# Three edits at the two edges of a hash-attention and MLP kernel: order and form of the projection requests, the buffer ring of the last output quarters, and wider unused products

## The chip, the cores and the metric

The kernel runs on one core of a Trainium2 chip. The metric is the device time of one execution in microseconds (us), median of several runs. In all the tables "trace" is one profiled execution; its span leaves out about 1.8 us that the timed figure has (898.2 against 899.9 for the kernel before), so spans are compared with spans and times with times.

## The reference, cut to what matters

```python
# q, k, v: (4, 8, 768, 64); proj: (64, 6); w_in: (512, 2048); w_out: (2048, 512); all float32
q_bits = (einsum('bhsd,dk->bhsk', q, proj) > 0)
k_bits = (einsum('bhsd,dk->bhsk', k, proj) > 0)
mask   = bucket(q_bits)[:, :, :, None] == bucket(k_bits)[:, :, None, :]
attn   = softmax(where(mask, q @ k.T / sqrt(64), -1e9))
x      = (attn @ v) -> (3072 tokens, 512)
out    = relu(x @ w_in) ** 2 @ w_out
```

The kernel goes through 16 pairs of heads and then through the two large products in chunks of tokens. The change touches only the first 12 us (the first pair's way from DRAM to its first scores) and the last 12 us (the way of the last output block to DRAM).

## The kernel before

The first loads and the start of the program. `nc.sync` is SyncE (SP), `nc.scalar` ScalarE (ACT), `nc.vector` VectorE (DVE), `nc.gpsimd` GpSimd (POOL); a `dma_start` on one of them is a request that this engine's sequencer issues.

```python
def load_first():
    for src, name in ((q, "q_nat"), (k, "k_nat")):
        t = p_qk.tile([P, SB, 2, D], FP32, name=name)
        for h, queue in enumerate((nc.sync, nc.scalar)):
            queue.dma_start(out=t[:, :, h], in_=src[0, h].rearrange("(t p) d -> p t d", t=SB))
        if src is q:
            nc.scalar.dma_start(
                out=projs[:, 0:NBITS],
                in_=proj.rearrange("(o d) n -> o d n", o=1).to_broadcast([2, D, NBITS]),
            )
        nat[0, name] = t

def keep_busy(n, w=512):            # products that nobody reads: they hold TensorE's clock up
    for _ in range(n):
        nc.tensor.matmul(out=void[:, 0:w], lhsT=busy[:, 0:P], rhs=busy[:, 0:w], start=True, stop=True)

# ... (cut)
load_first()
keep_busy(8)
# ... (constants, further loads: cut)
first_features(0, 0)                # TensorE transposes of the queries, copy out of PSUM
first_features(0, 1)
keep_busy(2, 256)
first_features(1, 0)                # transposes of the keys, first half
hash_bits(0, turn("hash"), (0,))    # needs projs
signs(0, 0)
first_keys(0, turn("hash"))
first_features(1, 1)
keep_busy(4)
```

The last outputs. `put_out` serves all output blocks but one; `put_last` serves the two quarters of the last block, which is finished after everything else.

```python
def put_out(i, ih, jh, n, o):
    ot = p_y.tile([P, HN], FP32, name="ot", bufs=2)
    nc.vector.transpose(out=ot, in_=o)
    # ... (cut)
    for a in range(P // 32):
        queue = nc.gpsimd if (ih, jh) == (1, 1) else nc.sync
        if (i, ih, jh) == (NCHUNK - 1, 1, 0) and a % 2:
            queue = nc.gpsimd
        queue.dma_start(out=out[at, ...], in_=ot[a * 32:(a + 1) * 32]...)   # cut

def put_last(n, o):
    row, col = n // 2, n % 2
    # ... (two TensorE transposes into PSUM: tp; cut)
    ot = p_y.tile([P, HN], FP32, name="ot", bufs=2)[:, 0:QN]
    if col:
        nc.scalar.copy(out=ot, in_=tp)
    else:
        nc.vector.tensor_copy(out=ot, in_=tp)
    # ... (cut)
    (nc.sync if col else nc.scalar).dma_start(out=out[lo:lo + QN, ...], in_=ot...)
```

## Time and profile before

| mark in the trace of before | us |
|---|---|
| time, median of 3 runs (range) | 899.87 (899.56 to 900.54) |
| span of the trace | 898.2 |
| first key transposes start on TensorE | 8.47 |
| first hash product | 8.91 |
| first score product | 12.28 |
| last TensorE work (transposes of the last quarters) starts | 887.93 |
| last copy starts, on DVE | 892.92 |
| GpSimd's closing drain ends | 895.37 |
| last store lands | 895.98 |

Read it as two edges around a full middle. TensorE computes nothing that counts before the keys are there, and after the last transposes another 10.3 us (898.2 - 887.93) pass in copying, storing and closing. "First score product" is the best mark for the front: a delay ahead of it moves all that follows. "Span minus start of the last transposes" is the best mark for the back.

### The profile page before, as it was taken

How to read it: one execution, taken by the hardware profiler on the slowest of the kernel's cores; microseconds unless marked ns; L12 is line 12 of the kernel's file. 1: busy time of each engine (PE TensorE's matmuls, PEld its weight loads, DVE VectorE, ACT ScalarE, POOL GpSimd, SP SyncE). 2: the span in 40 equal slices, each digit the busy share in tenths (PEclk: the TensorE clock that was granted, in tenths of full speed). 3: DMA queues.
4: the chain of work that ended last, by engine and by line, in shares of the span. 5: the costliest groups of instructions: out<-in, count | busy, mean ns of one | idle time of the engine just before them, and what ended most of it. 6: DMA issues, size and time to landing. Idle time of an engine off the chain costs nothing.

```text
span 898.2 us, 11774 instructions
## 1 busy us (share of the span) xinstructions
PE 878.5 (98%) x4296; PEld 502.8 (56%) x4296; DVE 711.0 (79%) x991; ACT 376.6 (42%) x609; POOL 91.7 (10%) x148
## 2 busy tenths in 40 slices
PE   8999999999999999999999999999999999999994
PEld 3444444444444444444688854446888544458883
DVE  4899999998999986888778775568777755777784
ACT  4988878887888861222211112222111122221110
POOL 2000000000000000554000111112001111100002
PEclk9999999999999999999999999999999999999998
DMA  9577879898976325999855744447757344445564
GB/s 180 104 149 145 198 176 208 166 274 204 265 158 159 107 100 205 292 267 288 314 171 154 180 85 141 128 148 274 242 153 191 63 144 152 153 138 156 152 180 81
DMA packets 219969, 158.14 MB, mean 176 GB/s; under 512 B 163746, under 2 KB 180642, under 8 KB 219906
## 3 DMA queue, kind: packets, MB, share of 16 engines
q1 hardware_dynamic: 186752, 84.04, 38.8%
q10 hardware_dynamic: 22418, 37.76, 13.9%
q0 software_dynamic: 10736, 35.53, 13.1%
q8 instruction: 36, 0.59, 0.3%
q14 instruction: 27, 0.22, 0.1%
HBM read 119.28 MB, written 38.01 MB: 175 GB/s over the span
## 4 chain that ended last, share of the span: by engine, by line
PE 90%; DVE 4%; DMA 3%; ACT 1%; issue 1%; SPq 0%; DVEq 0%; ACTq 0%
PE acc L688 58%; PE st L397 16%; PE xo L426 13%; PE tot L445 2%; PE hash L347 2%; DMA out_dram<-ot 1%; DVE total L416 1%; DMA raw<-in_moe_w_out_dram 1%; ACT bits L357 1%; DMA k_nat<-in_k_dram 1%; DVE peaks L729 0%; DVE b L778 0%; DVE ot L842 0%; DVE h L777 0%; DVE b_t L504 0%
## 5 line engine op out<-in xcount | busy, mean ns | idle before, releaser
L688 PE MATMUL acc<-x,w_unit 128*128 128x512 f32 x384 | 169.3, 592 | 0.0
L401 ACT ACTIVATE e<-st 128x1024 f32<-128x1024 f32 x192 | 145.2, 810 | 49.6 <-PE st L397 45.2
L397 PE MATMUL st<-feat,feat 64*128 64x512 f32 (+1 forms) x768 | 150.3, 483 | 0.0
L426 PE MATMUL xo<-e,v_nat 128*64 128x512 f32 (+1 forms) x768 | 134.8, 492 | 0.0
L688 PE MATMUL acc<-b,leaf 128*128 128x256 f32 x600 | 132.9, 379 | 0.0
L688 PE MATMUL acc<-t_x,w_unit 128*128 128x512 f32 x288 | 127.8, 593 | 0.0
L688 PEld LDWEIGHTS acc<-x,w_unit 128*128 128x128 f32 x384 | 72.9, 190 | 90.5 <-issue 89.9
L688 PEld LDWEIGHTS acc<-b,leaf 128*128 128x128 f32 x600 | 114.0, 190 | 16.8 <-issue 1.4
L416 DVE TENSOR_TENSOR total<-total,e 128x1536 f32<-128x1536 f32 x58 | 101.9, 1757 | 3.8
L426 PEld LDWEIGHTS xo<-e,v_nat 128*64 128x64 f32 x768 | 51.4, 136 | 82.4 <-issue 74.9
L688 PEld LDWEIGHTS acc<-t_x,w_unit 128*128 128x128 f32 x288 | 54.5, 190 | 69.7 <-issue 67.5
L397 PEld LDWEIGHTS st<-feat,feat 64*128 64x128 f32 x768 | 66.0, 188 | 33.9 <-issue 25.3
L777 DVE TENSOR_TENSOR h<-acc,two 128x512 f32<-128x512 f32 x24 | 16.6, 691 | 83.9 <-PE acc L688 83.8
L695 ACT COPY two<-acc 128x512 f32<-128x512 f32 (+1 forms) x45 | 21.9, 487 | 132.7 <-PE acc L688 116.8
L688 PE MATMUL acc<-t,leaf 128*128 128x256 f32 x336 | 76.5, 380 | 0.3 <-DVE t L504 0.3
L357 ACT ACTIVATE bits<-hash,lifts 32x384 bf16<-32x384 f32 x124 | 71.0, 573 | 7.6 <-PE hash L347 4.4
L695 ACT COPY one<-acc 128x512 f32<-128x512 f32 (+1 forms) x45 | 21.9, 487 | 113.1 <-PE acc L688 63.6
L688 PEld LDWEIGHTS acc<-t,leaf 128*128 128x128 f32 x336 | 63.6, 190 | 9.8 <-DVE t L504 1.1
L778 DVE SCALAR_TENSOR_TENSOR b<-h 128x512 f32<-128x512 f32 x96 | 64.3, 690 | 2.5
L397 PE MATMUL st<-bits,bits 64*128 64x256 bf16 (+1 forms) x384 | 63.1, 325 | 2.1 <-ACT e L401 1.2
L688 PE MATMUL acc<-b_t,leaf 128*128 128x256 f32 x240 | 54.5, 380 | 1.8 <-issue 1.8
L688 PEld LDWEIGHTS acc<-b_t,leaf 128*128 128x128 f32 x240 | 45.3, 190 | 9.0 <-issue 3.0
(127 smaller groups left out, 869.1 us busy)
## 6 DMA issues: line engine op xcount, KB each, us to landing
leaf<-w_out ACTq DMA_DIRECT2D x142, 256.0 KB, 3.0
w_unit<-w_in SPq DMA_DIRECT2D x24, 896.0 KB, 4.7
raw<-in_moe_w_in_dram SPq DMA_DIRECT2D x16, 512.0 KB, 5.6
raw<-in_moe_w_out_dram SPq DMA_DIRECT2D x16, 512.0 KB, 4.6
w_out<-sums POOLq DMA_DIRECT2D x16, 448.0 KB, 7.1
v_nat<-in_v_dram SPq DMA_DIRECT2D x16, 384.0 KB, 4.3
x_all<-x_t SPq DMA_DIRECT2D x16, 384.0 KB, 3.0
x<-x_all POOLq DMA_DIRECT2D x3, 2048.0 KB, 12.1
```

The source lines that it names most:

```text
L347: nc.tensor.matmul(out=banks[g * NR_B:(g + 1) * NR_B, h, 0:HS], lhsT=projs[rows], rhs=feat[pr, w][rows, c * HS:(c + 1) * HS], start=True, ...
L357: nc.scalar.activation(out=t[h * D:h * D + NR_B, c * HS:(c + 1) * HS], in_=hashed[pr, w][at, h, 0:HS], func=ACTF.Sign, scale=HUGE, bias=li ...
L397: nc.tensor.matmul(out=st[:, h, 0:hi - lo], lhsT=src[pr, 1][rows, key], rhs=src[pr, 0][rows, lo:hi], start=first, stop=not first,)
L401: nc.scalar.activation(out=e[:, :, lo:hi], in_=st[:, :, 0:hi - lo], func=ACTF.Exp, scale=scale)
L416: nc.vector.tensor_tensor(out=totals[pr], in0=totals[pr], in1=weights[pr, kt][:, :, 0:S], op=ALU.add)
L426: nc.tensor.matmul(out=xo[h * D:(h + 1) * D, lo:hi], lhsT=nat[pr, "v_nat"][:, h, kt * D:(kt + 1) * D], rhs=weights[pr, kt][:, h, lo:hi], s ...
L445: nc.tensor.matmul(out=tot[g * 32:(g + 1) * 32, 0:HS], lhsT=ones, rhs=src[:, h, c * HS:(c + 1) * HS], start=src is srcs[0], stop=src is sr ...
L688: nc.tensor.matmul(out=acc[to], lhsT=a(i), rhs=b(i), start=first and i == 0, stop=last and i == n - 1, skip_group_check=True,)
L695: nc.scalar.copy(out=t, in_=acc[of])
L777: nc.vector.tensor_tensor(out=h, in0=one, in1=two, op=ALU.add)
L778: nc.vector.scalar_tensor_tensor(out=out[:, r], in0=h, scalar=0.0, in1=h, op0=ALU.max, op1=ALU.mult)
```

## The change

It has three parts: the projections are asked for behind the keys, one plain 64 x 6 request on each of the two queues in place of one broadcast request on ACT's; the two unused products between queries and keys are 512 columns wide instead of 256; the last two output quarters take their buffers from another ring, which is idle by then.

```diff
-            if src is q:
-                nc.scalar.dma_start(
-                    out=projs[:, 0:NBITS],
-                    in_=proj.rearrange("(o d) n -> o d n", o=1).to_broadcast([2, D, NBITS]),
-                )
             nat[0, name] = t
+        for h, queue in enumerate((nc.sync, nc.scalar)):
+            queue.dma_start(out=projs[h * D:(h + 1) * D, 0:NBITS], in_=proj)
...
-        keep_busy(2, 256)
+        keep_busy(2)
...
-            ot = p_y.tile([P, HN], FP32, name="ot", bufs=2)[:, 0:QN]
+            ot = p_r.tile([P, HN], FP32, name="h", bufs=3)[:, 0:QN]
```

## The prediction

> **What bounds the kernel now.** I read the page first (busy shares, then the chain of work that ended last), then the chain in order of time, then the timeline of the first 12 us and the last 30 us, because the diff touches nothing in between.
>
> ```profile
> span 898.2 us, 11774 instructions
> PE 878.5 (98%) x4296; PEld 502.8 (56%) x4296; DVE 711.0 (79%) x991; ACT 376.6 (42%) x609; POOL 91.7 (10%) x148
> PE 90%; DVE 4%; DMA 3%; ACT 1%; issue 1%; SPq 0%; DVEq 0%; ACTq 0%
> ```
>
> TensorE is the bound: busy in 98% of the span and 90% of the chain. A change that takes no product away can only gain where TensorE has not begun yet or has already ended, so the two edges are what matters. The chain in order of time shows both edges:
>
> ```profile
> 2.67 5.66 DMA k_nat<-in_k_dram
> 8.47 0.52 PE tp L310 x3
> ...
> 887.45 0.59 DVE o L828 x2
> 888.04 4.80 DMA out_dram<-ot
> 892.92 0.42 DVE ot L866
> ```
>
> At the front one transfer, half of the first pair's keys, holds the whole program until 8.47 us. At the back the program waits 4.8 us for an output transfer before one 0.42 us copy. The timeline of the front (start, duration, engine, line; "ACTq" is an issue of a transfer by ScalarE's sequencer):
>
> ```profile
> 1.29 0.53 SPq L270 DMA_DIRECT2D k_nat<-in_k_dram  x1
> 1.50 1.14 ACTq L274 DMA_DIRECT2D projs<-in_proj_dram  x1
> 2.67 0.39 ACTq L270 DMA_DIRECT2D k_nat<-in_k_dram  x1
> 6.15 0.63 PE L327 MATMUL xo<-busy 128*128 128x256 bf16 x2
> 8.47 0.52 PE L310 MATMUL tp<-ident,k_nat 128*128 128x128 f32 x3 [1.69 <-DMA k_nat<-in_k_dram]
> ```
>
> SP asks for its half of the keys at 1.29 us. ACT asks for the other half only at 2.67 us, because it asks for the projections first, and that one request takes 1.14 us of issuing. TensorE is through with the queries and the two unused products at 6.78 us (6.15 + 0.63) and is idle 1.69 us until the ACT half has landed. From issue to landing, by the list of transfers (KB, us): the SP half 4.5 us, so at 5.8; the ACT half 5.7 us, so at 8.35.
>
> ```profile
> k_nat<-in_k_dram SPq DMA_DIRECT2D x1, 192.0 KB, 4.5
> k_nat<-in_k_dram ACTq DMA_DIRECT2D x1, 192.0 KB, 5.7
> ```
>
> The back:
>
> ```profile
> 887.93 0.77 PE L859 MATMUL acc<-ident,o 128*128 128x128 f32 x4 [1.09 <-DVE o L828]
> 888.40 0.37 ACT L864 COPY ot<-acc 128x256 f32<-128x256 f32 x1 [5.47 <-PE acc L859]
> 888.80 0.39 SPq L868 DMA_DIRECT2D out_dram<-ot  x1
> 892.92 0.42 DVE L866 COPY ot<-acc 128x256 f32<-128x256 f32 x1 [4.72 <-DMA out_dram<-ot]
> 893.38 0.40 ACTq L868 DMA_DIRECT2D out_dram<-ot  x1
> ```
>
> The last two output quarters take the same path (transpose on TensorE, copy out of PSUM, store), one through ACT and SP, one through DVE and ACT. The first finds a free buffer. The second draws the ring of two "ot" buffers round to the one that the transposed block of 886.40 us still occupies, and whose last piece GpSimd asked for only at 888.04; it lands at 892.85, and the copy starts at 892.92 although its input was ready at 888.70 (887.93 + 0.77).
>
> **What the Trainium skill says.** (1) "DMA: Bandwidth & Descriptors", section "Why a DMA increments its semaphore by 16 and not by 1": the slowest dimension of both sides decides over how many of the 16 DMA engines a transfer is spread; "Rules for kernel authors" there warns that a leading broadcast of c copies confines it to c engines. The old projection request has a leading broadcast of 2, so 128 descriptors of 24 bytes would sit on two engines, ahead of the keys in ACT's queue; the new ones have 64 partitions outermost, 4 descriptors for each engine. No view here shows engines singly, but the 1.14 us issue (0.39 to 0.53 for the larger ones) and the 5.7 against 4.5 us of the two key halves agree. (2) Same page, "Issuing engines are not separate DMA queues": asking from two queues saves issue time only, since both share the 16 engines. So I expect earlier requests, not more bandwidth. (3) "TensorE: Matmul & The Clock Gate", Part 1: the array runs at half clock until it has been busy for about 3.4 us, in a free-running window. The trace agrees:
>
> ```profile
> L310 PE MATMUL tp<-ident,q_nat x6: 421/421/421, 4.9 to 5.9; 128*128 128x128 f32 x6
> L310 PE MATMUL tp<-ident,k_nat x6: 272/273/330, 8.5 to 10.7; 128*128 128x128 f32 x6
> ```
>
> The transposes of the queries, to 6.36 us, ran at the low clock (421 ns), those of the keys from 8.47 at the high one (272 ns); the change of clock fell between. (4) "DMA: Bandwidth & Descriptors", "Anatomy of one DMA": about 2 us of a small transfer is fixed, mostly the receipt of the write. Here the 128 KB store that ran alone took 2.6 us, and the one at 888.80 that shared the engines took 4.2.
>
> **The change, part by part.**
>
> Projections behind the keys. ACT's key request moves from 2.67 to about 1.3 us, beside SP's. Bandwidth: the two queries and two key halves are 4 x 192 KB = 786 kB; the list of rates shows up to 285 GB/s while both queues carry such rows, from about 2.05 us on. 786 / 275 = 2.9 us, so the last byte comes at about 4.95; the queries landed 0.65 to 1.1 us after their last bytes by the same count, so both key halves land at about 5.6 to 6.0 us, against 8.35. The projections, 3 KB, follow in both queues and should land by 6.5. They are wanted by the hash, after the key transposes, so they get no wait of their own unless they land after about 7.4.
>
> Two unused products of 512 columns in place of 256. At the low clock one takes about 0.43 us (eight took 3.59 at 1.48 us), so TensorE is through at 6.15 + 0.86 = 7.0 instead of 6.6 us. They now become what the keys wait for: key transposes at 7.0 instead of 8.47, 1.47 us earlier. They are there so that the clock is up by then; if it rises later, three transposes at double spacing cost 0.25 us more and the first hash about as much. I take 0.15 off: front gain 1.3 us. It stays: from there each step of the first pair waits for compute (ACT signs, exponentials, DVE sums), not for a transfer, and the first idle time that a transfer ends, the weights at 204.5 us, is counted from an SP request that itself waited for DVE. Everything moves up together.
>
> Quarters in the ring "h". That ring (three buffers) was last used by the gates long before, and the built program confirms that the two copies keep only their wait for TensorE; the two pieces of SP and of GpSimd drop out of it. The DVE copy moves from 892.92 to about 888.75, its store from 893.38 to about 889.2, 4.1 us earlier. Not all of it counts: the GpSimd piece still lands at 892.85 and SP's store at 888.80 + 4.2 = 893.0, and the new store shares the engines with both. Its 128 KB at some 180 GB/s is 0.7 us more, so the last landing is at 893.0 to 893.7 instead of 895.98 (893.38 + 2.6). After the last landing come 2.2 us (898.2 - 895.98) of closing semaphores, unchanged. Gain 2.3 to 2.9 us, if nothing else ends later.
>
> Sum: 1.3 + 2.5 = 3.8 us.
>
> **The rivals.**
>
> Rival A: GpSimd's closing drain sets the new end.
>
> ```profile
> L1254 POOLq DRAIN  x3: 40/113/6670, 888.7 to 897.9; - x3
> ```
>
> The first of these begins at 888.7 and lasts 6.67 us, to 895.37. I do not know what ends it. If it follows GpSimd's own transfers, the change leaves it where it is; the closing exchange then takes the 0.8 us from 897.4, where GpSimd's closing semaphores begin, to 898.2, the end is at 896.2 before the front gain, and the back gain is 2.0 and not 2.7. For it: its start depends on nothing that the change moves. Against it: it may end with the last store of all. I give it a half, hence 2.5 in the sum. Time if true: 896.6.
>
> Rival B: the keys gain little, because the projections or the pair-1 loads now stand in the way. For it: one wait for the projections is now on both queues, and SP asks for 96 KB loads from about 2.3 us on. Against it: those are behind the keys in SP's queue, and the projections are small and spread. Front gain 0.7; time 896.7.
>
> Rival C: the clock is still low at 7.0 us, and stays so for up to a microsecond more, since the window runs free. Front gain 0.8; time 896.6.
>
> Rival D: both edges give their best (1.5 and 2.9): 895.5.
>
> Rival E: a gap of the front is taken up later, where something not moved sets the pace. Against it: after 340 us the chain is products of TensorE nearly without a gap, and before it each wait is relative. Time 897.4 with only the back gain.
>
> **Range and chances.** 899.87 - 3.8 = 896.1 us, taking the difference of spans as the difference of times. The three runs of before lie within 1.0 us, so I widen beyond D and B: 895.0 to 897.4. 2% is 18 us, more than both edges together hold (8.5 us ahead of the keys, some 10 us after the last product), so faster by 2% has 0.005 and slower, for which I see no mechanism, 0.005.
>
> **What would show it.** Right: ACT's key request at about 1.3 us and both halves landed by about 6; key transposes starting at 6.8 to 7.2 us right behind the unused products, with no wait for a transfer; the hash without one for the projections; the DVE copy at about 888.8 less the front gain, waiting for TensorE; the last landing about 2.5 us earlier against the last product. The step on the clock is judged by the 421 or 272 ns of the key transposes. The drain of GpSimd, its end counted from the copy of L864, decides between A and my first sum. Wrong would be: a wait of more than 0.3 us for the projections or the keys after 7.2 us, a middle stretch that is longer than before, or a time outside 895.0 to 897.4.

## The result

The changed kernel takes 895.67 us (median of 6 runs, 894.87 to 896.34), the kernel before in the same rounds 899.65 us (897.04 to 900.54). The ratio is 0.9958, with an interval of 0.9945 to 0.9972. Here and below a ratio is the mean time of one kernel's runs over that of the other's runs in the same rounds, so it isn't quite the ratio of the medians. The spans of the two traces differ by 4.3 us (898.2 - 893.9).

The page of the changed kernel, span and shares of the chain:

```profile
span 893.9 us, 11767 instructions
...
PE 92%; DVE 4%; DMA 1%; ACT 1%; issue 1%; SPq 0%; ACTq 0%; DVEq 0%
```

The transfers' share of the chain fell from 3% to 1%, but not by the change alone. The 4.8 us output transfer at the back has left the chain. About half of the fall is a weights transfer of 7.60 us at 204.5 us, in the middle stretch that is examined below. The keys are still on the chain, now from 1.29 to 6.64 us instead of 2.67 to 8.33:

```profile
1.29 5.35 DMA k_nat<-in_k_dram
6.69 0.55 PE tp L307 x3
```

The front in the timeline (start, duration, engine, line, count, and in brackets the idle time before it with what ended it):

```profile
1.29 0.67 ACTq L270 DMA_DIRECT2D k_nat<-in_k_dram  x1
...
5.78 0.59 PE L324 MATMUL xo<-busy 128*128 128x512 bf16 x2
...
6.69 0.55 PE L307 MATMUL tp<-ident,k_nat 128*128 128x128 f32 x3 [0.31 <-DMA k_nat<-in_k_dram]
...
7.26 1.46 PE L344 MATMUL hash<-feat,projs 64*32 64x384 f32 x12
```

ACT asks for its half of the keys at 1.29 instead of 2.67 us. The wait of 1.69 us has shrunk to 0.31. The unused products are through at 6.37 (5.78 + 0.59), the keys come at 6.69, and the hash follows the key transposes (6.69 + 0.55 = 7.24) without a gap. The transfers of this front (KB, us from issue to landing):

```profile
k_nat<-in_k_dram ACTq DMA_DIRECT2D x1, 192.0 KB, 5.4
...
projs<-in_proj_dram SPq DMA_DIRECT2D x1, 1.5 KB, 5.3
```

So ACT's keys land at 6.7 (1.29 + 5.4), and projections of 1.5 KB need 5.3 us behind the keys (ahead of them, in an experiment below, 3.1 to 3.4): asked for at 1.87 and 2.00, they land at 7.2 to 7.3, with nothing to spare before the hash. The back:

```profile
885.57 0.77 PE L856 MATMUL acc<-ident,o 128*128 128x128 f32 x4 [1.09 <-DVE o L825]
...
886.38 0.42 DVE L863 COPY h<-acc 128x256 f32<-128x256 f32 x1 [0.53 <-PE acc L856]
```

The DVE copy waits for TensorE alone, 0.53 us, where it waited 4.72 us for a store. Its own store is asked for at 886.83. GpSimd's closing drain, in the list of instructions by line (shortest, median and longest in ns; first and last start):

```profile
L1251 POOLq DRAIN  x3: 40/112/6770, 886.3 to 893.7; - x3
```

Its long instance, 6.77 us from 886.3, ends at 893.07, and the span ends 0.83 us later. In the kernel before it ended at 895.37, only 0.6 us ahead of the last landing. Now the two lie further apart: the last landing is at about 891.0 (886.83 + 4.2), and the drain is what comes last.

Where the 4.3 us of the two traces came from, by the marks:

| stretch | before | after | difference |
|---|---|---|---|
| start to first score product | 12.28 | 10.53 | 1.75 |
| from there to the first product of the second block | 327.91 | 327.22 | 0.69 |
| from there to the last transposes | 547.74 | 547.82 | -0.08 |
| from there to the end | 10.27 | 8.33 | 1.94 |

The 0.69 us in the middle is examined below; it isn't the change's.

### The profile page after: what moved, and what is told of

The parts are those of the page before. It is cut to its first block, busy times and chain, and to the rows that moved or that the text cites. A ratio compares the mean times of both kernels' runs of the same rounds, so it can differ in the third digit from the quotient of the medians.

```text
span 893.9 us, 11767 instructions
## 1 busy us (share of the span) xinstructions
PE 878.5 (98%) x4296; PEld 502.5 (56%) x4296; DVE 710.9 (80%) x991; ACT 376.0 (42%) x609; POOL 91.5 (10%) x148
## 4 chain that ended last, share of the span: by engine, by line
PE 92%; DVE 4%; DMA 1%; ACT 1%; issue 1%; SPq 0%; ACTq 0%; DVEq 0%
PE acc L685 58%; PE st L394 17%; PE xo L423 14%; PE tot L442 2%; PE hash L344 2%; DVE total L413 1%; DMA k_nat<-in_k_dram 1%; ACT bits L354 1%; DMA out_dram<-ot 0%; DVE peaks L726 0%; DVE b L775 0%; DVE ot L839 0%; DVE h L774 0%; DVE b_t L501 0%; ACT e L398 0%
```

## The experiments

My theory after the result: the front gains because ACT's keys are asked for earlier, which comes from the short issue of the new request as much as from its place; the back gains 2 us because the wait for a buffer is gone, and would gain more if GpSimd's drain did not end last. Rivals: the unused products (through the clock) make the front's gain; the back's gain is the whole gain and the front's is absorbed; the end follows the last store, not the drain. Twelve runs, of ten new kernels and the two known ones, were made in three groups on three chips. All gave correct results, and all the timed runs were in the fast state; the single look at the kernel before has no state. The last column of the table gives the two marks of the edges, from one trace of each kernel.

| kernel | median us (before, same rounds) | ratio (95%) | first score product; last transposes to end |
|---|---|---|---|
| last ring alone | 897.70 (899.98) | 0.9969 (0.9956 to 0.9981) | 12.94; 8.41 |
| projections alone | 898.44 (899.98) | 0.9980 (0.9967 to 0.9993) | 10.77; 10.18 |
| wide products alone | 899.32 (899.98) | 0.9988 (0.9976 to 0.9999) | 12.21; 10.41 |
| old request, behind the keys | 898.24 (899.98) | 0.9981 (0.9968 to 0.9994) | 11.06; 10.22 |
| full change again | 895.90 (900.33) | 0.9949 (0.9936 to 0.9961) | 10.88; 8.45 |
| full change, narrow products | 896.34 (900.33) | 0.9954 (0.9941 to 0.9967) | 10.41; 8.36 |
| full change, ACT stores for GpSimd | 894.64 (900.33) | 0.9946 (0.9932 to 0.9959) | 10.60; 7.01 |
| three ideas together | 893.54 (900.33) | 0.9922 (0.9910 to 0.9935) | 10.73; 7.05 |
| eight wide products, before | 898.69 (900.26) | 0.9988 (0.9971 to 1.0004) | 12.54; 10.55 |
| new request, ahead of the keys | 898.02 (900.26) | 0.9982 (0.9966 to 0.9997) | 10.53; 10.63 |
| three ideas, no unused products | 892.83 (900.26) | 0.9916 (0.9902 to 0.9930) | 9.73; 6.72 |
| before again, one look | 899.59 | (single run, state unknown) | 13.33; 10.37 |

**The last ring alone.** The kernel before with the last part of the change only:

```diff
-            ot = p_y.tile([P, HN], FP32, name="ot", bufs=2)[:, 0:QN]
+            ot = p_r.tile([P, HN], FP32, name="h", bufs=3)[:, 0:QN]
```

> The kernel before with only the last quarters in the ring h. Theory of the drain: the DVE copy follows the transposes at once (about 888.8 us instead of 892.9) and the last store lands 2 to 3 us earlier, but GpSimd's closing drain keeps its start (888.7) and its 6.7 us, so it ends at about 895.4 and the span at 896.2: gain 2.0 us, about 897.7 us, ratio 0.9978. Theory that the last store alone sets the end: last landing about 893.3 plus 2.2 us, span 895.5, gain 2.7 us, ratio 0.9970. Theory that the wait only moves elsewhere: under 0.5 us.

Its ratio is 0.9969, so 2.8 us. In the trace the stretch after the last transposes is 8.41 us, as in the full change and 1.86 less than before; the drain ends at 895.15 and the span 0.85 later. So the back's gain stands by itself and is bounded by the drain. The span is 2.2 us shorter than that of before: 1.86 at the back, 1.0 in the middle (0.63 of it ahead of the second block, examined below), and 0.66 lost at the front, where nothing was edited and yet the first score product came at 12.94 instead of 12.28. The reason is in the front of this trace:

```profile
8.11 0.87 PE L310 MATMUL tp<-ident,k_nat 128*128 128x128 f32 x3 [2.41 <-DMA k_nat<-in_k_dram]
```

Three key transposes took 0.87 us where they took 0.52 in before. The view by stretches (us; busy time of TensorE, its weight loads, DVE, ACT, POOL, each with a count; granted clock, the share of full speed that TensorE was allowed; DMA share; GB/s) says why, first for this kernel:

```profile
8.00:10.00 2.00, 1.89 (x13) 0.89 (x15) 0.56 (x1) 0.00 (x0) 0.00 (x0) 0.50 1.56 143
```

and then for the kernel before:

```profile
8.00:10.00 2.00, 1.53 (x15) 0.60 (x15) 0.56 (x1) 0.11 (x1) 0.00 (x0) 1.00 1.34 133
```

In the idle stretch of 2.41 us, 2.2 us after its start, the granted clock fell to half, where it stayed from about 7.9 to 11.3 us, and this run did 13 products in these two microseconds where the other did 15. Here TensorE was through with queries and unused products at 5.70 us, against 6.78 in before (its clock had risen sooner: six query transposes took 0.82 us against 1.49), and so waited longer for keys that came at nearly the same time. What it won early, it lost again at half clock. (The view shows a clock of 1.00 from the start in every trace here, though the first eight products plainly ran slow. So the low clock of the first microseconds is read from durations, and only the later falls from the records.)

**The kernel before again.** To see whether that was chance, the unchanged kernel was looked at a second time.

> The kernel before once more, for its trace: from the first sign activation to the first product of the second block 328.8 us if the weights of 204 us happen to land in time, up to 330.3 if not; half clock after the keys if the window falls badly, not otherwise; back edge as before: 10.2 to 10.4 us from the last transposes to the end.

```profile
8.48 0.52 PE L310 MATMUL tp<-ident,k_nat 128*128 128x128 f32 x3 [1.94 <-DMA k_nat<-in_k_dram]
...
8.93 2.21 PE L347 MATMUL hash<-feat,projs 64*32 64x384 f32 x12
...
13.33 0.39 PE L397 MATMUL st<-bits,bits 64*128 64x512 bf16 x2
```

The same program, with the keys at the same time (8.48 against 8.47), waited 1.94 us instead of 1.69, ran at half clock from about 9.6 to 13.0, took 2.21 us for a hash that takes 1.5, and reached its first score product 1.05 us later. So the kernel before has two fronts, 12.3 and 13.3 us, by chance. The Trainium skill ("TensorE: Matmul & The Clock Gate", section "Why this matters for your kernels") advises to leave no gaps over about 3 us between bursts of products, since one window of idle puts the clock back to half. The clock records here agree on the half clock, and both spells of it lasted 3.41 us; but they came with only 1.94 and 2.41 us of idle, and with 1.69 us in a third run there was none. The length of the idle time can't be the whole rule: in this run the clock fell at 9.57 us, when TensorE had been busy again for 1.09 us. What decides between the cases was not tested. In none of the nine traces of kernels with early keys did the clock drop after the queries: their idle ahead of the keys was 1.11 us at most.

**The projections alone.** The first part of the change on the kernel before.

```diff
-            if src is q:
-                nc.scalar.dma_start(out=projs[:, 0:NBITS], in_=...to_broadcast([2, D, NBITS]))
+        for h, queue in enumerate((nc.sync, nc.scalar)):
+            queue.dma_start(out=projs[h * D:(h + 1) * D, 0:NBITS], in_=proj)
```

> The kernel before with only the projections asked for behind the keys on both queues (unused products 256 wide as before). Theory of the request order: ACT's key half is asked for at 1.3 us and lands at about 6.6, key transposes start at about 6.7 instead of 8.5, gain 1.5 to 1.8 us, ratio about 0.9982; TensorE waits some 0.3 us longer for the keys than in the full change, nothing else differs. Rival, that the wider unused products carry part of it by lifting the clock: key transposes at 421 ns and a gain of 1.0 us or less.

It takes 0.9980 of the time before, 1.8 us, and its first score product comes at 10.77, against 12.28 or 13.33. The back is as before (10.18 against 10.27). The front's gain is real by itself; with the ring's 2.8 us it makes 4.6 us, and the full change makes 3.8 us in the first measurement and 4.6 us (0.0051 x 900) in its repeat below. Within the intervals, about 1.1 us to each side, the two edges add, and no absorption of the front's gain is to be seen. The first key transposes did run at low clock here (three took 0.90 us, against 0.55 in the full change), the sign that the rival had named, but the gain isn't the 1.0 us or less that it expected with that sign.

**Old request behind the keys, and new request ahead of them.** The first part changes two things at once: the place of the request and its form. One kernel moves the old broadcast request behind the keys:

```diff
-            if src is q:
-                nc.scalar.dma_start(out=projs[:, 0:NBITS], in_=...to_broadcast([2, D, NBITS]))
             nat[0, name] = t
+        nc.scalar.dma_start(out=projs[:, 0:NBITS], in_=...to_broadcast([2, D, NBITS]))
```

> The kernel before with the old single broadcast request for the projections, but placed behind the keys on ACT's queue. If the order of the requests is all that matters: the keys land at about 6.6 us, gain 1.5 us, ratio 0.9983. If the form matters too (128 small pieces on few engines, 1.14 us to issue): the projections land clearly after the keys (later than 7.5 us), the first hash waits for them, and the gain is 0.3 to 1.0 us.

The other keeps the old place and takes the new form:

```diff
             if src is q:
-                nc.scalar.dma_start(out=projs[:, 0:NBITS], in_=...to_broadcast([2, D, NBITS]))
+                for h, queue in enumerate((nc.sync, nc.scalar)):
+                    queue.dma_start(out=projs[h * D:(h + 1) * D, 0:NBITS], in_=proj)
```

> The kernel before with the projections still asked for ahead of the keys, but in the new form, one request of 64 rows on each queue. If the form alone does it (short issue, spread pieces): ACT's keys are asked for at about 1.9 instead of 2.67 us and land at about 7.1, SP's 0.6 later than before at 6.4: key transposes at about 7.1, gain 1.2 to 1.4 us, nearly that of the full front. If it is the order: keys land after 8 us, gain under 0.4 us.

The old request behind the keys:

```profile
8.30 0.87 PE L346 MATMUL hash<-feat,projs 64*32 64x384 f32 x12 [0.74 <-DVE feat L318]
```

The keys were transposed from 7.01 on, but the hash began only at 8.30: TensorE stood 0.74 us. The profile puts the wait down to the DVE copy of the keys, which ended at 8.15. But the first hash products use the queries alone: in the changed kernel they start at 7.26, when that copy had not even begun. So what they waited for is the projections, whose request was issued from 1.99 to 3.13 us. (This is inferred: the list of transfers gives no landing for this one.) The new request ahead of the keys:

```profile
2.07 0.59 ACTq L270 DMA_DIRECT2D k_nat<-in_k_dram  x1
...
10.53 0.39 PE L395 MATMUL st<-bits,bits 64*128 64x512 bf16 x2 [0.46 <-ACT bits L355]
```

Its two projection requests took 0.54 and 0.58 us of issue instead of 1.14, ACT's keys were asked for at 2.07 and landed 4.2 us later, at 6.3, *earlier* than in the full change, where they were asked for at 1.29 and needed 5.4 us. SP's half came later instead, and it is the half that TensorE waited for:

```profile
2.12 0.82 SPq L270 DMA_DIRECT2D k_nat<-in_k_dram  x1
...
k_nat<-in_k_dram SPq DMA_DIRECT2D x1, 192.0 KB, 4.5
...
6.72 0.52 PE L308 MATMUL tp<-ident,k_nat 128*128 128x128 f32 x3 [1.11 <-DMA k_nat<-in_k_dram]
```

Both halves were there at 6.6 to 6.7 us, as in the full change. The projections took 3.4 us at most. The first score product is at 10.53, the same as in the full change. In time the two are alike (0.9981 and 0.9982, both some 1.7 us), and like the projections alone (0.9980), so the times don't tell the three apart. (For the old request behind the keys 0.3 to 1.0 us was expected: the wait for the projections came, the smaller gain didn't show in the time.) In the traces, one of each, the form of the request is enough for the gain, the order alone gets less at the mark (11.06), and both together get no more than the form; but the full change's own two traces lie at 10.53 and 10.88. Asking for ACT's keys 0.8 us sooner did not bring the last half of the keys sooner: 6.7 us in both. And "form" is itself two things: the broadcast is gone, and the rows are split over two queues. The two new requests take 1.12 us of issue together, as much as the old one's 1.14, but side by side on SP and ACT. A split request that keeps the broadcast, or a plain one on ACT alone, was not run, so which of the two helps stays open.

**The wide products alone**, in the kernel before:

```diff
-        keep_busy(2, 256)
+        keep_busy(2)
```

> The kernel before with only the two unused products widened from 256 to 512 columns. Theory of the request order: the keys still land at about 8.35 us, TensorE is idle 1.3 instead of 1.7 us before them, gain 0.0 us, ratio 1.000. Rival (clock): the clock is up earlier and the first pair runs faster, gain 0.3 us or more.

The ratio is 0.9988 with an interval that ends at 0.9999, and the mark at the front is 12.21, 0.07 from that of before. A mean gain of a microsecond fits a kernel that no longer falls to half clock in some of its runs (its idle ahead of the keys was 1.46 us, and the clock held), but one trace and this interval don't show it.

**Eight wide products** in their place were to fill nearly the whole wait:

```diff
-        keep_busy(2, 256)
+        keep_busy(8)
```

> The kernel before with eight unused products of 512 columns where it has two of 256, enough to keep TensorE busy nearly until the keys land at 8.35 us. The trace of ring_only showed the clock granted at half from 7.9 to 11.3 us, after 2.4 us of idle before the keys; before itself did not show it. Theory that the wait for the keys sometimes costs the clock: no half clock after the keys in this run, mean 0.3 to 0.8 us under before, and a narrower spread than before has. Theory that the half clock is rare or costs nothing: within 0.3 us of before. If the eight end after the keys have landed (clock low throughout): up to 0.4 us slower.

The idle ahead of the keys was 1.06 us, the clock held, the first score product came at 12.54, and the ratio is 0.9988 (0.9971 to 1.0004): unclear. How often the kernel before runs at half clock, and so what unused products are worth there on average, stays open.

**The full change again, and with the narrow products.** The first is the changed kernel unedited; the second is it with

```diff
-        keep_busy(2)
+        keep_busy(2, 256)
```

> The full change once more, as the yardstick for the other three runs on this chip. About 3.8 us under before, ratio 0.9958; GpSimd's closing drain starts at about 886.3 us, lasts 6.7 to 6.8 us and ends 0.8 us before the span does. Any middle stretch (from the first sign activation to the first product of the second block) between 328.8 and 330.3 us, as in the traces so far, would be chance of the transfers.

> The full change with the two unused products put back from 512 to 256 columns. Theory that the width does nothing once the keys come early: same time as the full change within 0.3 us; TensorE idle about 0.7 instead of 0.3 us before the keys, clock not falling since that gap is short. Rival, that the wider products are what keeps the clock up: in some runs the half clock lasts over the first hash (key transposes at 421 ns), mean 0.4 to 0.8 us slower and a wider spread than the full change.

The repeat measured 0.9949 and the narrow one 0.9954, medians 895.90 and 896.34, with intervals that overlap nearly whole. In the repeat the clock was still low during the unused products (0.81 us for two), and the keys began at 7.04 right behind them; in the narrow one the products took 0.38 us and the keys began at 6.57. The narrow one's first score product is earlier by 0.47 us (10.41 against 10.88), which the times don't show. The second part of the change does nothing measurable once the keys come early.

The repeat also settles the middle stretch. DVE's wait for a weights transfer in it and in the kernels before and after is given in brackets, in the timeline near 210 us; first before:

```profile
212.12 0.43 DVE L141 TENSOR_SCALAR power<-raw 128x512 uint32<-128x512 uint32 x1 [1.53 <-DMA raw<-in_moe_w_out_dram]
```

and then the repeat:

```profile
210.61 0.43 DVE L141 TENSOR_SCALAR power<-raw 128x512 uint32<-128x512 uint32 x1 [1.34 <-DMA raw<-in_moe_w_out_dram]
```

The wait was 1.53 us in one trace of the kernel before and nothing in the other; it was 0.70 us in one trace of the changed kernel and 1.34 in the other. One program shows both, so the 0.69 us that the middle of the first pair of traces differs by is chance and not the change.

**ACT stores for GpSimd's last two.** The full change, with the two pieces of the last `put_out` that GpSimd asked for given to ACT:

```diff
                 if (i, ih, jh) == (NCHUNK - 1, 1, 0) and a % 2:
-                    queue = nc.gpsimd
+                    queue = nc.scalar
```

> The full change with the two pieces of the last transposed block that GpSimd stored now stored from ACT's queue, so that GpSimd comes to its closing drain some 2.5 us earlier. Theory that the drain takes about 6.7 us from when GpSimd arrives and has been the end: it starts at about 883.8, ends at about 890.5, and the end is again the last landing (about 891) plus 2.2 us: span about 893.2, 0.7 us less than the full change. If the drain is tied to the other engines' stores or ends: it grows to end at the same 893.1 and nothing is gained. If ACT's issuing delays its own copy: the last stores come up to 0.5 us later and the time stays or rises.

```profile
L1251 POOLq DRAIN  x3: 40/113/5295, 882.7 to 891.8; - x3
```

The long drain begins at 882.7, takes 5.3 us instead of 6.8 and ends at 888.0, more than 4 us ahead of the end. The last store lands at about 890.15 (issued at 886.35, 3.8 us), and the span ends 1.95 us after it, like the 2.2 us of the kernel before. So the drain was what came last in the full change, and without it the end follows the last landing again. From the last transposes to the end it is 7.01 us instead of 8.33 to 8.45: 1.3 to 1.4 us, about twice the 0.7 us that I had worked out. Of the 1.32 against the first trace, 0.9 is the drain's: had the end of the full change followed its last landing, 5.46 us after the transposes, by the same 1.95, it would have been 7.41 (by the 2.2 us of the kernel before, 7.7, and the drain's part 0.7). The other 0.4 is ACT's last store, which took 3.8 us instead of 4.2 in this trace. In time the gain is less clear: the median is 1.26 us below that of the full change, but one run of 897.88 us lifts the mean, and the ratios (0.9946 and 0.9949) hardly differ.

What does the drain follow? In four traces (before, after, its repeat, the ring alone) it ended 2.5 us after GpSimd's own last store had landed: 892.85 and 895.37 in before, 890.6 and 893.07 in after. In this kernel and the next it is 3.1 us. That it waits for GpSimd's own transfers and then for something of 2.5 to 3.1 us fits all six; what this something is, no run shows. It doesn't wait for all stores: in before and in this kernel it ended ahead of the last landing.

**Three ideas together.** On top of the last kernel: the first pair's keys asked for in halves, the projections between them; one unused product instead of two; the transposed blocks of the last chunk in the ring "h" and the last quarters back in "ot".

```diff
+        ask(q, "q_nat", 0, SB)
+        ask(k, "k_nat", 0, HB)          # SB = 6 blocks of 128 rows, HB = 3
         for h, queue in enumerate((nc.sync, nc.scalar)):
             queue.dma_start(out=projs[h * D:(h + 1) * D, 0:NBITS], in_=proj)
+        ask(k, "k_nat", HB, SB)
...
-        keep_busy(2)
+        keep_busy(1)
...
-            ot = p_y.tile([P, HN], FP32, name="ot", bufs=2)
+            ring, bufs = ((p_r, "h"), 3) if i == NCHUNK - 1 else ((p_y, "ot"), 2)
+            ot = ring[0].tile([P, HN], FP32, name=ring[1], bufs=bufs)
...
-            ot = p_r.tile([P, HN], FP32, name="h", bufs=3)[:, 0:QN]
+            ot = p_y.tile([P, HN], FP32, name="ot", bufs=2)[:, 0:QN]
```

> A try at beating both: the pieces on ACT, the keys of the first pair asked for in two halves with the projections between them, one unused product before them, and the transposed output blocks of the last chunk in the ring h (three buffers), the last quarters in the old ring. Front: the first hash at about 6.6 instead of 7.3 us (0.6). Back: VectorE no longer idle 2.9 us before a transposed block, last product chain up to 0.6 us earlier, and 0.7 us of the drain. Sum 1.9 us under the full change, about 893.8 us, if the smaller key requests do not slow the front; under 0.7 us if only the drain counts.

It is the fastest of its group, 893.54 us, but two of the three ideas did nothing visible here. The first score product came at 10.73, no earlier than in the full change: the keys were there, but TensorE still had its unused product to do at the low clock and came to them at 6.58. And DVE, in its transposes of the last chunk, still waited 1.92 us for a store (2.85 in the full change, 2.36 in the kernel above, 2.71 in the one below), three buffers or not. I had taken the number of buffers for the cause of that wait; it isn't, or not alone, and the true one was not looked for further.

**The same without unused products ahead of the keys:**

```diff
-        keep_busy(1)
+        keep_busy(0)
```

> The best version without the unused product ahead of the first half of the keys, which had landed at 5.4 us while TensorE came free for it only at 6.6 us. Front: first half of the key transposes at about 6.2, first hash at about 6.7 to 6.9 instead of 7.36 us: 0.5 us under the best version, about 893.1 us; if the clock then rises one window later (key transposes and hash at half clock): no gain or 0.5 us slower.

```profile
5.94 0.49 PE L314 MATMUL tp<-ident,k_nat 128*128 128x128 f32 x3
```

The keys are transposed right behind the queries, and the hash starts at 6.36, right behind the keys; TensorE waits for no transfer at all. The first score product comes at 9.73, 0.8 us before that of the full change. The time is 892.83 us (892.07 to 893.51), ratio 0.9916: 7.6 us less than the kernel before, against 3.8 to 4.6 for the change under study. It is the fastest version measured, and it beats the kernels before and after; over the version with one product its lead isn't shown, since the intervals nearly coincide and in its trace the clock also rose sooner (query transposes in 1.24 us against 1.50).

## Why the prediction was right

The time, 895.67 us, lies 0.4 us from the predicted 896.1 and inside the range; "within 2%" came true. The sum of 3.8 us is the 0.42% of the ratio (3.8 us of 900), and its terms hold in part.

*Keys asked for at 1.3 us:* right. *Both halves landed by 6:* SP's did (5.8), ACT's came at 6.7. The 275 GB/s was too good: the changed kernel moved 287 GB/s from 3 to 4 us, but 224 in the next microsecond and 202 in the half after it. This is the weakest figure of the working. The prediction also took the 5.7 us of ACT's keys against SP's 4.5 as a sign that the old request, ahead of them, was confined to few engines. It isn't one: with nothing but the queries ahead, ACT's half took 5.4 us in the full change and 5.7 in its repeat. On how many engines the old request lay, no view shows. *Projections landed by 6.5:* wrong by 0.7 to 0.8 us, for the same reason; it cost nothing only because they were wanted at 7.24. Rival B was nearer than the prediction had it, and the kernel with the old request behind the keys is rival B come true, with a gap of 0.74 us.

*Unused products through at 7.0, keys then:* right in the repeat (7.04), where the clock was low; in the first trace the clock had risen during the queries, they were through at 6.37, and the keys came last by 0.31 us. So the deduction of 0.15 us for a low clock was not needed. Rival C, a long spell at low clock after the change, didn't occur.

*Front gain 1.3 us:* a term too small. The pair of traces gives 1.75, the projections alone 1.8 in time, and two traces of each kernel give anything from 1.40 (12.28 - 10.88) to 2.80 (13.33 - 10.53). The 1.40 is the repeat, which ran as the prediction had it, at low clock up to the keys; the first trace won more because its clock rose sooner (query transposes in 1.07 us against 1.49). What is missing in the prediction is a cost of the kernel *before*: in some of its runs the wait for the keys comes with half clock as well, about one microsecond. I had looked for a falling clock only in the kernel after.

*Credit for the order of the requests:* the prediction named both the form (the issue of 1.14 us) and the place, and counted the gain on the place, "from 2.67 to about 1.3". The new form in the old place gives the same mark. That the requests start earlier was right; that an earlier start brings the keys earlier by as much was not.

*Everything moves up together:* right. The middle stretch kept its length but for a chance wait.

*The back:* rival A is what happened. The DVE copy moved as predicted, to just behind TensorE, and the new end is the drain's end plus 0.8 us, as worked out there. It gave 1.94 us where A said 2.0. The sum had taken 2.5 as the mean of two cases (half of 2.0 and 2.7 would be 2.35), so it was 0.5 too high here as it was 0.5 too low at the front; the two errors cancelled, and that is luck, and part of why the total came so near. A was argued "for" with a start that nothing moves; the kernels with fewer GpSimd stores fit its other thought, that the drain follows GpSimd's own transfers.

## What to carry to other kernels

At the edges of a program that is bound by one engine, write down every thing that ends there, with its time, before removing the last: here a drain that ended 0.6 us ahead of the last store became the end when that store moved, and took back 0.7 to 0.9 us of a possible 2.6 to 2.9. Look at how long a small request holds its queue before reordering it: one of 1.14 us became two of 0.54 to 0.58 us side by side, and that alone gave the front's gain. And look at when things land, not at when they are asked for. Look at the kernel before at least twice: a wait of about 2 us sometimes comes with half clock too, and a single trace shows only one of the two cases.

## What the Trainium skill lacked or had wrong

- "TensorE: Matmul & The Clock Gate": the advice of no gaps over about 3 us (section "Why this matters for your kernels") was too generous here. Idle stretches of 1.94 and 2.41 us each came with 3.41 us at half clock (hash 2.21 us instead of 1.5 to 1.6); 1.69 us did not.
- No page says that GpSimd's closing drain can last microseconds (5.3 to 6.9 us here). It ended 2.5 us (four traces) or 3.1 us (two) after GpSimd's own last store had landed, and where it came last the span ended 0.83 us after it. Two stores moved from GpSimd to ACT shortened the tail by 1.3 to 1.4 us.
- "DMA: Bandwidth & Descriptors" (section "Rules for kernel authors") says what a leading broadcast does to the spread over the engines, but not how the issue time follows from the shape of a request: 128 rows of 24 bytes in one request with a broadcast of 2 took 1.14 us of ACT's sequencer, 64 such rows without one 0.53 to 0.58 us, and a key half of 192 KB 0.39 to 0.82 us.
